# Three of four attention score blocks moved behind the expert-weight product, into the gate/value banks

## The chip, the cores and the metric

The kernel runs on one core of one Trainium2 chip. The metric is the time of one execution on the device, in microseconds. Engines are named as in the profile: PE is TensorE (PEld its weight loads), DVE VectorE, ACT ScalarE, POOL GpSimd, SP SyncE, which here issues the transfers.

## The reference

Two attentions and a SwiGLU layer. Inputs are q, k, v of 8 batches, 8 heads, 576 tokens, 64 dimensions, and p of 32 packed rows per head. All is fp32.

```python
def sm_attn(qq, kk, vv):
    s = scale * np.matmul(qq, kk.transpose(0, 1, 3, 2))
    a = np.exp(s - np.max(s, axis=-1, keepdims=True))
    return np.matmul(a / (np.sum(a, axis=-1, keepdims=True) + 1e-09), vv)
p_packed = sm_attn(p, k, v)              # first attention: 32 rows over 576 keys
out = sm_attn(q, p_packed, p_packed)     # second attention: 576 rows over 32 keys
x = out.transpose(0, 2, 1, 3).reshape(4608, 512)
g = x @ w_gate                           # 512 x 1536
result = (g * sigmoid(g) * (x @ w_val)) @ w_out   # 1536 x 512
```

## The kernel before

**Algebra.** The second attention is never multiplied out. With the weights `a2` of the second attention (576 tokens by 32 packed rows per head), gate and value are `a2` times the product of the packed rows with the gate and value weights. That product, called M, is small and is made once for each batch and each pair of chunks of the 1536 inner columns (`m_mm`). Gate and value (`gv_chunk`), and the output product (`out_mm`), run in fp32r with each operand split into a high and a low word: three matmuls replace one. The split of M is a cast on ACT (`mh`, line 513) and a subtraction on DVE that reads the same PSUM bank again (`ml`, line 487).

**Stages.** Batch 0 runs from a list of words written by hand (`PROGRAM`), with its own order. Batches 1 to 7 run in a loop (line 807). For batch b it goes through 12 chunks `fc` of 128 inner columns. In each chunk the tokens come in two parts: A (256) and B (320). A chunk writes, on PE:

1. A: gate tile, value tile (six matmuls each, line 544);
2. if `fc` is odd, M for the next pair of chunks (lines 201 and 517; in chunk 11, M of the next batch);
3. the output matmuls of the previous chunk's A (six, line 564), absent in chunk 0;
4. B: gate tile, value tile;
5. the output matmuls of the previous chunk's B, absent in chunk 0.

A counter (`fill`, line 821) steps at each tile and at each group of three output matmuls: 1 and 2 are A's two tiles, 3 and 4 the outputs of A, 5 and 6 B's tiles, 7 and 8 the outputs of B. M is written at count 2.

Beside PE, each part goes through silu of the gate tile (ACT, line 551), the product with the value tile `hf` (DVE, 556; for B also `t`, 559), a cast `hh` (ACT, 107) and a subtraction `hl` (DVE, 113).

**Attention of the next batch.** While batch b runs, the attentions of d = b + 1 are made by the generator `aux_of`. It takes a step at counts 4 and 8 of every chunk but chunk 0. The first attention (`q_scores`, `q_weights`) has two blocks of scores, g = 0 and 1, each 32 matmuls into two banks. Each bank is read by a maximum and a subtraction (lines 335 and 336). Then follow the exponential (339), sums, a gather of maxima and sums through DRAM (`zd`, then `x`), the common factor, a transpose of the weights, and the product with v (`q_pack`, 395). The second attention has two blocks of scores too (`s2_mm`), one for each half of the tokens, each 16 matmuls into two banks, read by two transposes (421). Each half then has maximum and subtraction (441, 442), exponential (446), sums (453 to 455), scaling (459), a transpose (468), a cast (471) and a subtraction (475), which give `a2` in two words.

Before the change the four blocks of scores are written at chunk 1 count 4, chunk 2 count 4, chunk 7 count 4 and chunk 7 count 8. Each stands between output matmuls and B, or between output matmuls and the next A.

**Banks.** PSUM has three pools: `acc` (four banks, the outputs), `gv` (two banks, gate and value tiles in turn) and `aux` (two banks: M, all scores, the packed product, and the outputs of the remaining tokens of two batches). In the loop `ps()` gives an `aux` bank.

**Order of the queues.** PE's order is the written order. On the other engines the compiler orders the instructions by when it takes them to be ready. An instruction that went through `pin` (line 91) is kept behind the instruction written just before it on its engine; one that did not may be issued earlier or later than where it is written. The attention's DVE instructions and exponentials are pinned. `hf`, `hh`, `hl`, silu, the casts `mh` and the low words `ml` are not. The exponentials are put in a list `late` and written behind the next silu.

Of the kernel before, what the change touches and what calls it, by code (L numbers as in the profile page):

```python
# [59 lines left out]
def tile_pack_attention_swiglu(ctx: ExitStack, tc: tile.TileContext, qT, kT, v, vq, pT, wgv, wout, out):  # L60
# [30 lines left out]
    def pin(ins):  # L91

        return tc.keep_in_program_order(ins) if steady[0] else ins

    late = []

    def ps():
        turn[0] += 1
# [210 lines left out]

    sq = {}  # L310

    def q_scores(b):


        k_t, p_t = kps[b]
        e = pool.tile([P, NPAR, NHP, NKQ * NP], F32, tag="s2", bufs=1, name="e1")
        z = pool.tile([P, 2, NPAR, NHP], F32, tag="z1", bufs=2, name="z1")
        sq[b] = (e, z)
        nc.gpsimd.memset(e[:, :, :, SQ:], 0.0)
        for g in range(2):  # L320
            pss = [ps(), ps()]
            for i in range(2):
                for j in range(NJ):
                    for par in range(NPAR):
                        r = slice(64 * par, 64 * par + 64)
                        nc.tensor.matmul(  # L326
                            pss[par][NP * j : NP * j + NP, i * SQ : (i + 1) * SQ],
                            p_t[r, 2 * g + i, :],
                            k_t[r, j // 2, 2 * g + i, j % 2 * SQ : j % 2 * SQ + SQ],
                            start=True, stop=True,  # L330
                        )
            hs = slice(2 * g, 2 * g + 2)
            for par in range(NPAR):
                x, m = pss[par][:, : 2 * SQ].rearrange("p (h n) -> p h n", h=2), z[:, 0, par, hs]
                pin(nc.vector.tensor_reduce(m, x, axis=AX.X, op=ALU.max))
                pin(nc.vector.tensor_tensor(
                    e[:, par, hs, :SQ], x, m.unsqueeze(2).broadcast_to([P, 2, SQ]), op=ALU.subtract
                ))
            late.append(lambda hs=hs: pin(nc.scalar.activation(e[:, :, hs, :SQ], e[:, :, hs, :SQ], AF.Exp, scale=SCALE)))
            yield  # L340
            if g == 0:
                yield

    def q_weights(b):


        e, z = sq[b]
        for g in range(2):
            if g:
                yield  # L350
            hs = slice(2 * g, 2 * g + 2)
            pin(nc.vector.tensor_reduce(z[:, 1, :, hs], e[:, :, hs, :SQ], axis=AX.X, op=ALU.add))
        zv = z.rearrange("p s r h -> p s (r h)")
        x = pool.tile([P, NJ, 2, H], F32, tag="x1", bufs=1, name="x1")
        zd = dram.tile([P, 2, H], F32, tag="zd", bufs=2, name="zd")
        nc.sync.dma_start(zd, zv)
        for i in range(NJ):
            nc.sync.dma_start(x[NP * i : NP * i + NP], zd.rearrange("(j n) s h -> n j s h", j=NJ))
        for _ in range(2):
            yield  # L360
        y = pool.tile([P, 3, NJ + 1, H], F32, tag="pp", bufs=1, name="y1")
        m, t, f = y[:, 2, 0], y[:, 2, 1], y[:, 2, 2]
        pin(nc.vector.tensor_reduce(m, x[:, :, 0].rearrange("p j h -> p h j"), axis=AX.X, op=ALU.max))
        pin(nc.vector.tensor_tensor(
            y[:, 0, :NJ], x[:, :, 0], m.unsqueeze(1).broadcast_to([P, NJ, H]), op=ALU.subtract
        ))
        pin(nc.vector.tensor_tensor(y[:, 0, NJ], zv[:, 0], m, op=ALU.subtract))
        late.append(lambda: pin(nc.scalar.activation(y[:, 0], y[:, 0], AF.Exp, scale=SCALE)))
        yield
        pin(nc.vector.tensor_tensor(y[:, 1, :NJ], y[:, 0, :NJ], x[:, :, 1], op=ALU.mult))  # L370
        pin(nc.vector.tensor_reduce(t, y[:, 1, :NJ].rearrange("p j h -> p h j"), axis=AX.X, op=ALU.add))
        pin(nc.vector.tensor_scalar(f, t, 1e-9, None, op0=ALU.add))
        pin(nc.vector.reciprocal(t, f))
        pin(nc.vector.tensor_tensor(f, t, y[:, 0, NJ], op=ALU.mult))
        yield
        a1 = pool.tile([P, NPAR, NHP, NKQ, NP], F32, tag="a1", bufs=1, name="a1")
        for par in range(NPAR):
            w = e[:, par, :, :SQ]
            pin(nc.vector.tensor_tensor(
                w, w, f[:, NHP * par : NHP * par + NHP].unsqueeze(2).broadcast_to([P, NHP, SQ]), op=ALU.mult  # L380
            ))
            pin(nc.vector.transpose(
                a1[:, par].rearrange("p h k n -> p (h k n)"), e[:, par].rearrange("p h n -> p (h n)")
            ))
            yield
        sq[b] = a1

    def q_pack(b):
        a1, v_t = sq.pop(b), vs.pop(b)
        p_p = ps()  # L390
        for hp in range(NHP):
            for k in range(NKQ):
                for g in range(P // NP):
                    par, ds = g // 2, slice(g % 2 * NP, g % 2 * NP + NP)
                    nc.tensor.matmul(  # L395
                        p_p[NP * g : NP * g + NP, NP * hp : NP * hp + NP],
                        a1[:, par, hp, k, :], v_t[:, par, hp, k, ds],
                        start=(k == 0), stop=(k == NKQ - 1),
                    )
        ppts[b] = pool.tile([P, P], F32, tag="ppt", bufs=2, name="ppt")  # L400
        pin(nc.vector.transpose(ppts[b], p_p[:, :P]))
# [6 lines left out]

    two = {}

    def s2_mm(b, c):
        two[b, c] = [ps(), ps()]
        q_t, ppt = qs[b], ppts[b]
        by_head(
            [x[:, :HS] for x in two[b, c]], lambda r, hp: ppt[r, 32 * hp : 32 * hp + 32],
            lambda r, hp: q_t[r, c, hp],
        )

    def s2_block(b, c):
        for par in range(NPAR):  # L420
            pin(nc.vector.transpose(st2[b][0][:, c, par], two[b, c][par][:, :HS]))

    def s2_scores(b):
        for c in range(2):
            s2_mm(b, c)
            s2_block(b, c)
            yield

    def s2_view(b, cs):
        s2, r2 = st2[b]  # L430
# [53 lines left out]

    def m_lows():
        while lows:
            nc.vector.tensor_tensor(*lows.pop(0), op=ALU.subtract)  # L487

    m_ps = {}

# [26 lines left out]
    def m_part(b, k, fcs):  # L517
        m_mm(b, k, fcs)
        m_high(b, k, fcs)
        m_lows()  # L520

    t4 = {}

# [3 lines left out]
        split(hh, hl, src, hi, lo)  # L527
        return hh, hl

    def gv_chunk(b, fc, is_b, fill):  # L530
        odd = b % 2
        n = NB if is_b else NA
        off = (0 if odd else 256) if is_b else (320 if odd else 0)
# [15 lines left out]
            fill()  # L549
        sg = pool.tile([P, NB], F32, tag="sg", bufs=1, name="sg")  # L550
        nc.scalar.activation(sg[:, :n], pgs[0][:, :n], AF.Silu)  # L551
        if late:
            late.pop(0)()
        hf = pool.tile([P, 256], F32, tag="hf", bufs=2, name="hf")
        o, o4 = (64, 0) if is_b and odd else (0, 256)
        nc.vector.tensor_tensor(hf, pgs[1][:, o : o + 256], sg[:, o : o + 256], op=ALU.mult)  # L556
# [19 lines left out]

    both = slice(0, 2)

    def aux_of(b):

        d = b + 1
        if d == B:
            return
        yield from q_scores(d)
        yield from q_weights(d)
        if d + 1 < B:
            load_k(d + 1)
        q_pack(d)
        yield
        yield  # L590
        if d < B - 1:
            load_v(d + 1)
        s2_tiles(d)
        yield from s2_scores(d)
        if d < B - 1:
            load_q(d + 1)
        s2_a2(d)
        order = (1, 0) if d % 2 else (0, 1)
        halves = [slice(c, c + 1) for c in order]
        first, second = halves  # L600
        s2_max(d, first)
        late.append(lambda: s2_exp(d, first))
        yield
        s2_sums(d, first)
        yield
        s2_max(d, second)
        late.append(lambda: s2_exp(d, second))
        yield
        s2_scale(d, first)
        low = s2_back(d, first.start)  # L610
        yield
        low()
        s2_sums(d, second)
        yield
        s2_scale(d, second)
        low = s2_back(d, second.start)
        yield
        low()

    with tc.manual_schedule(engines={mybir.EngineType.PE}):  # L620
        warm_ps = ps_aux.tile([P, 512], F32, tag="aux", name="warm_ps")
# [184 lines left out]
        steady[0] = True  # L806
        for b in range(1, B):
            rows, accs = begin(b)
            aux = aux_of(b)
            ha, hb = {}, {}  # L810

            def outs(fc, which, fill):
# [5 lines left out]
            for fc in range(NFC):  # L818
                count = [0]

                def fill():
                    count[0] += 1
                    if count[0] == 2:
                        if fc == NFC - 1 and b + 1 < B:
                            run_all(aux)
                            m_part(b + 1, 0, both)
                        elif fc % 2 and fc + 1 < NFC:
                            m_part(b, (fc + 1) // 2, both)
                    if b == 1 and 1 <= fc <= 6 and count[0] == 7:
                        wout_high(fc + 5)  # L830
                        wout_low(fc + 5)
                    if fc and count[0] in (4, 8):
                        next(aux, None)

                ha[fc] = gv_chunk(b, fc, False, fill)
                if fc:
                    outs(fc - 1, 0, fill)
                hb[fc] = gv_chunk(b, fc, True, fill)
                if fc:
                    outs(fc - 1, 1, fill)  # L840
            run_all(aux)
            outs(NFC - 1, 0, lambda: None)
            outs(NFC - 1, 1, lambda: None)
            end(rows, accs)
# [46 lines left out]
```

## Time and profile before

| What | Value |
|---|---|
| median of 3 runs | 759.64 us (758.2 to 760.34) |
| profiled execution, whole | 760.24 us |
| profiled execution, span of its instructions | 758.5 us |
| PE busy | 745.1 us (98%) |
| PEld busy | 590.6 us (78%) |
| DVE busy | 456.6 us (60%) |
| ACT busy | 369.6 us (49%) |
| bytes moved by DMA | 59.15 MB |
| granted clock of PE, mean | 0.996 |

The whole time includes what lies around the span. Busy times count each engine alone, and they overlap. A row of a timeline gives start, length, engine, line of the kernel, operation, the tile written and those read, and a count of merged instructions; what stands in brackets is the idle time of the engine before it and whom it waited for. A row of a group gives count, total busy time and mean nanoseconds of one, and then the idle time before them.

### The profile page before, as it was taken

To read this page: it belongs to the slowest core of one execution; us is meant where nothing else is said; L and a number is where in the kernel's file an instruction comes from. 1 tells how busy PE (TensorE), PEld (TensorE's weight loads), DVE (VectorE), ACT (ScalarE), POOL (GpSimd) and SP (SyncE) were. 2 spreads that over 40 slices of the span, in tenths; PEclk is the share of its full clock that TensorE was granted. 3 is DMA by queue.
4 is the path that set the end of the run, shared out by engine and by line. 5 is a ranking of instruction groups with operands and counts; after the bars stand their busy time and mean duration, and the time that the engine had idled before them with its cause. 6 is when DMAs were issued, how large, how long until landed. Compare 5 with 4: busy or idle time off the path is not lost.

```text
span 758.5 us, 15106 instructions
## 1 busy us (share of the span) xinstructions
PE 745.1 (98%) x6280; PEld 590.6 (78%) x6280; DVE 456.6 (60%) x1004; ACT 369.6 (49%) x662; POOL 2.0 (0%) x13
## 2 busy tenths in 40 slices
PE   7999999999999999998999999999999999999998
PEld 5756666787888878787788887878788787888886
DVE  5997977665756547454674556656475554743334
ACT  3777654653626436452443545464272642633331
POOL 0000000000000000000000000000000000000000
PEclk9999999999999999999999999999999999999999
DMA  9686582203011030122201221100101000010001
GB/s 355 242 319 249 207 313 78 67 3 133 1 70 67 4 134 1 56 69 71 64 29 42 69 72 63 43 15 3 71 2 69 2 3 2 1 56 1 1 1 70
DMA packets 20004, 59.15 MB, mean 78 GB/s; under 512 B 5984, under 2 KB 7008, under 8 KB 17376
## 3 DMA queue, kind: packets, MB, share of 16 engines
q1 hardware_dynamic: 19792, 58.12, 21.2%
q8 instruction: 49, 0.80, 0.4%
q14 instruction: 19, 0.16, 0.1%
q10 hardware_dynamic: 144, 0.07, 0.0%
HBM read 48.69 MB, written 9.49 MB: 77 GB/s over the span
## 4 chain that ended last, share of the span: by engine, by line
PE 95%; DVE 2%; ACT 1%; issue 1%; ACTq 0%
PE gv L544 36%; PE acc L564 30%; PE aux L201 8%; PE gv L721 6%; PE acc L747 5%; PE aux L564 4%; PE aux L395 1%; PE aux L326 1%; DVE ml L487 1%; PE acc L625 1%; PE warm_ps L625 1%; ACT mh L513 1%; PE gv_aux L201 0%; PE aux L277 0%; DVE w L133 0%
## 5 line engine op out<-in xcount | busy, mean ns | idle before, releaser
L551 ACT ACTIVATE sg<-gv 128x256 f32<-128x256 f32 (+1 forms) x168 | 68.9, 410 | 179.7 <-PE gv L544 145.4
L544 PE MATMUL gv<-a2h,ml 128*128 128x256 f32 (+1 forms) x672 | 148.4, 302 | 0.7
L544 PE MATMUL gv<-a2h,mh 128*128 128x256 f32 (+1 forms) x672 | 144.7, 297 | 0.4 <-issue 0.4
L544 PE MATMUL gv<-a2l,mh 128*128 128x256 f32 (+1 forms) x672 | 144.4, 296 | 0.0
L556 DVE TENSOR_TENSOR hf<-gv,sg 128x256 f32<-128x256 f32 x168 | 70.7, 421 | 120.6 <-PE gv L544 101.2
L564 PE MATMUL acc<-wo_h,hl 128*128 128x512 f32 x336 | 136.8, 407 | 0.0
L564 PE MATMUL acc<-wo_l,hh 128*128 128x512 f32 x336 | 132.4, 394 | 0.0
L564 PE MATMUL acc<-wo_h,hh 128*128 128x512 f32 x336 | 131.7, 392 | 0.0
L544 PEld LDWEIGHTS gv<-a2h,ml 128*128 128x128 f32 x672 | 113.9, 189 | 21.7 <-issue 7.6
L107 ACT CAST hh<-hf 128x256 fp32r<-128x256 f32 x168 | 67.9, 404 | 120.5 <-DVE hf L556 120.4
L113 DVE TENSOR_TENSOR hl<-hf,hh 128x256 fp32r<-128x256 f32 x168 | 71.0, 423 | 80.3 <-ACT hh L107 79.8
L544 PEld LDWEIGHTS gv<-a2h,mh 128*128 128x128 f32 x672 | 109.0, 191 | 0.6 <-issue 0.6
L544 PEld LDWEIGHTS gv<-a2l,mh 128*128 128x128 f32 x672 | 108.5, 190 | 0.0
L564 PEld LDWEIGHTS acc<-wo_h,hl 128*128 128x128 f32 x336 | 63.4, 189 | 42.5 <-issue 34.4
L564 PEld LDWEIGHTS acc<-wo_h,hh 128*128 128x128 f32 x336 | 63.3, 188 | 14.6
L564 PEld LDWEIGHTS acc<-wo_l,hh 128*128 128x128 f32 x336 | 63.4, 189 | 7.7
L487 DVE TENSOR_TENSOR ml<-aux,mh 128x512 fp32r<-128x512 f32 x92 | 59.0, 683 | 6.4 <-ACT mh L513 6.3
L201 PE MATMUL aux<-w,ppt 64*32 64x512 f32 (+1 forms) x784 | 52.4, 588 | 0.5 <-ACT mh L513 0.5
L513 ACT CAST mh<-aux 128x512 fp32r<-128x512 f32 x92 | 49.2, 588 | 3.6 <-PE aux L201 0.7
L747 PE MATMUL acc<-wo_f,h 128*128 128x512 f32 x96 | 44.2, 594 | 0.0
L551 ACT ACT_TABLE_LOAD x30 | 38.5, 1283 | 4.2 <-issue 3.6
L747 PEld LDWEIGHTS acc<-wo_f,h 128*128 128x128 f32 x96 | 17.3, 189 | 17.2 <-issue 15.7
(145 smaller groups left out, 756.0 us busy)
## 6 DMA issues: line engine op xcount, KB each, us to landing
st<-in_wgv SPq DMA_DIRECT2D x12, 1024.0 KB, 6.9
k_t<-in_kT SPq DMA_DIRECT2D x16, 576.0 KB, 4.9
q_t<-in_qT SPq DMA_DIRECT2D x16, 576.0 KB, 5.0
out<-ot SPq DMA_DIRECT2D x36, 256.0 KB, 2.1
v_t<-in_vq SPq DMA_DIRECT2D x6, 1280.0 KB, 5.7
st<-in_wout SPq DMA_DIRECT2D x6, 1024.0 KB, 7.2
v_t<-in_v SPq DMA_DIRECT2D x2, 1024.0 KB, 8.3
p_t<-in_pT SPq DMA_DIRECT2D x7, 64.0 KB, 2.5
```

The source lines that it names most:

```text
L107: e.copy(dst, src)
L113: lo.tensor_tensor(dst_l, src, dst_h.bitcast(F32), op=ALU.subtract)
L201: nc.tensor.matmul(outs[par][32 * hp : 32 * hp + 32], lhs(r, hp), rhs(r, hp), start=True, stop=True)
L487: nc.vector.tensor_tensor(*lows.pop(0), op=ALU.subtract)
L513: nc.scalar.copy(m[0][at], src)
L544: nc.tensor.matmul(pg[:, :n], m_[:, g, f, s * P : (s + 1) * P], a_[:, g, off : off + n], start=(i == 0), stop=(i == 5),)
L551: nc.scalar.activation(sg[:, :n], pgs[0][:, :n], AF.Silu)
L556: nc.vector.tensor_tensor(hf, pgs[1][:, o : o + 256], sg[:, o : o + 256], op=ALU.mult)
L564: nc.tensor.matmul(acc[:, :], h_[:, c : c + P], w_[fc // 2][:, fc % 2], start=(fc == 0 and i == 0), stop=(fc == NFC - 1 and i == 2),)
L625: nc.tensor.matmul(at[:, :P], ident, ident, start=True, stop=True)
L721: nc.tensor.matmul(held[i][s][:, :n], m_[:, g, f, s * P : (s + 1) * P], a_[:, g, off : off + n], start=(j == 0), stop=(j == len(todo) - 1),)
L747: nc.tensor.matmul(accs[2 * is_b + c], half(i)[:, c * P : c * P + P], wos[fc // 2][:, fc % 2], start=(fc == 0), stop=(fc == NFC - 1),)
```

## The change

The generator becomes a table: `plan_of(b)` says, for each chunk and place, what is written there. The places are the counts 2, 4 and 8, `"a"` (behind the silu of A), `"b"` (behind the silu of B) and `"m"` (behind the whole of A, so behind M on PE in odd chunks). The functions of the attention are cut into pieces, each written as before.

- The first block of the first scores moves to chunk 0, count 2. It stays in `aux`.
- The second moves to chunk 1, `"m"`, and takes its two banks from `gv`.
- The second attention's blocks move to chunk 7, `"m"` and chunk 9, `"m"`, and take their banks from `gv`. The order of its two halves on PE is now that of their use.
- `m_lows` (the subtractions `ml`) moves from behind M's casts to behind whatever stands at `"m"`, and is pinned.
- The exponentials move from B to A: chunks 1, 2, 4, 8 and 10. Sums, gather, common factor, the packed product's turn, maxima and the scaling of the second attention move by up to two chunks, as the table says. The loads of k and p are written at chunk 3 count 8 in place of chunk 6 count 4, that of v in the same chunk 7, that of q in chunk 9 in place of chunk 8.

```diff
+    def gv_ps():
+        return ps_gv.tile([P, 512], F32, tag="gv", name="gv_aux")
+
-    def q_scores(b):
+    def q_scores(b, g, bank=ps):
...
+        pss = [bank(), bank()]
...
-    def s2_mm(b, c):
-        two[b, c] = [ps(), ps()]
+    def s2_mm(b, c, bank=ps):
+        two[b, c] = [bank(), bank()]
...
     def m_lows():
         while lows:
-            nc.vector.tensor_tensor(*lows.pop(0), op=ALU.subtract)
+            pin(nc.vector.tensor_tensor(*lows.pop(0), op=ALU.subtract))
...
     def m_part(b, k, fcs):
         m_mm(b, k, fcs)
         m_high(b, k, fcs)
-        m_lows()
...
-    def gv_chunk(b, fc, is_b, fill):
+    def gv_chunk(b, fc, is_b, fill, behind):
...
-        if late:
-            late.pop(0)()
+        behind()
...
-    def aux_of(b):
...
+    def plan_of(b):
+        d, plan = b + 1, {}
+        def at(fc, place, *todo):
+            plan.setdefault((fc, place), []).extend(todo)
+        if d < B:
+            c, c2 = (1, 0) if d % 2 else (0, 1)
+            cs, cs2 = slice(c, c + 1), slice(c2, c2 + 1)
+            at(0, 2, lambda: q_scores(d, 0))
+            at(1, "a", lambda: q_exp(d, 0))
+            at(1, "m", lambda: q_scores(d, 1, gv_ps))
+            at(1, 8, lambda: q_sums(d, 0))
+            at(2, "a", lambda: q_exp(d, 1))
+            at(2, 8, lambda: q_sums(d, 1), lambda: q_gather(d))
+            at(3, 8, lambda: q_common(d))
+            if d + 1 < B:
+                at(3, 8, lambda: load_k(d + 1))
+            at(4, "a", lambda: q_common_exp(d))
+            at(4, 4, lambda: q_factors(d))
+            at(4, 8, lambda: q_turn(d, 0))
+            at(5, 8, lambda: q_turn(d, 1))
+            at(6, 4, lambda: q_pack(d))
+            if d + 1 < B:
+                at(7, "m", lambda: load_v(d + 1))
+            at(7, "m", lambda: s2_tiles(d), lambda: s2_a2(d))
+            at(7, "m", lambda: s2_mm(d, c, gv_ps), lambda: s2_block(d, c))
+            at(7, 8, lambda: s2_max(d, cs))
+            at(8, "a", lambda: s2_exp(d, cs))
+            at(8, 8, lambda: s2_sums(d, cs), lambda: s2_scale(d, cs), lambda: s2_turn(d, c), lambda: s2_high(d, c))
+            at(9, "m", lambda: s2_mm(d, c2, gv_ps), lambda: s2_block(d, c2))
+            if d + 1 < B:
+                at(9, "m", lambda: load_q(d + 1))
+            at(9, 4, lambda: s2_low(d, c))
+            at(9, 8, lambda: s2_max(d, cs2))
+            at(10, "a", lambda: s2_exp(d, cs2))
+            at(10, 8, lambda: s2_sums(d, cs2), lambda: s2_scale(d, cs2), lambda: s2_turn(d, c2))
+            at(10, 8, lambda: s2_high(d, c2))
+            at(11, 4, lambda: s2_low(d, c2))
+        return lambda fc, place: [f() for f in plan.pop((fc, place), ())]
...
                     count[0] += 1
                     if count[0] == 2:
+                        run(fc, 2)
                         if fc == NFC - 1 and b + 1 < B:
-                            run_all(aux)
                             m_part(b + 1, 0, both)
                         elif fc % 2 and fc + 1 < NFC:
                             m_part(b, (fc + 1) // 2, both)
...
-                ha[fc] = gv_chunk(b, fc, False, fill)
+                ha[fc] = gv_chunk(b, fc, False, fill, lambda: run(fc, "a"))
+                run(fc, "m")
+                m_lows()
                 if fc:
                     outs(fc - 1, 0, fill)
-                hb[fc] = gv_chunk(b, fc, True, fill)
+                hb[fc] = gv_chunk(b, fc, True, fill, lambda: run(fc, "b"))
```

More of the change, by code (lines that the diff above doesn't have):

```diff
@@ L93, in pin @@
         return tc.keep_in_program_order(ins) if steady[0] else ins
-    late = []
     def ps():
@@ L310, in tile_pack_attention_swiglu @@
     sq = {}
-    def q_scores(b):
+    def gv_ps():
+        return ps_gv.tile([P, 512], F32, tag="gv", name="gv_aux")
+    def q_scores(b, g, bank=ps):
         k_t, p_t = kps[b]
[L316 to L342, printed above, removed]
@@ L344, in q_weights @@
-    def q_weights(b):
-        e, z = sq[b]
[L348 to L353, printed above, removed]
+        if g == 0:
+            e = pool.tile([P, NPAR, NHP, NKQ * NP], F32, tag="s2", bufs=1, name="e1")
+            z = pool.tile([P, 2, NPAR, NHP], F32, tag="z1", bufs=2, name="z1")
+            sq[b] = [e, z]
+            nc.gpsimd.memset(e[:, :, :, SQ:], 0.0)
@@ new lines, in q_scores @@
+        e, z = sq[b]
+        pss = [bank(), bank()]
+        for i in range(2):
+            for j in range(NJ):
+                for par in range(NPAR):
+                    r = slice(64 * par, 64 * par + 64)
+                    nc.tensor.matmul(
+                        pss[par][NP * j : NP * j + NP, i * SQ : (i + 1) * SQ],
+                        p_t[r, 2 * g + i, :],
+                        k_t[r, j // 2, 2 * g + i, j % 2 * SQ : j % 2 * SQ + SQ],
+                        start=True, stop=True,
+                    )
@@ new lines, in q_scores, with q_exp @@
+        hs = slice(2 * g, 2 * g + 2)
+        for par in range(NPAR):
+            x, m = pss[par][:, : 2 * SQ].rearrange("p (h n) -> p h n", h=2), z[:, 0, par, hs]
+            pin(nc.vector.tensor_reduce(m, x, axis=AX.X, op=ALU.max))
+            pin(nc.vector.tensor_tensor(
+                e[:, par, hs, :SQ], x, m.unsqueeze(2).broadcast_to([P, 2, SQ]), op=ALU.subtract
+            ))
+    def q_exp(b, g):
+        x = sq[b][0][:, :, 2 * g : 2 * g + 2, :SQ]
+        pin(nc.scalar.activation(x, x, AF.Exp, scale=SCALE))
@@ L354, in q_weights, with q_sums, q_gather @@
+    def q_sums(b, g):
+        e, z = sq[b]
+        hs = slice(2 * g, 2 * g + 2)
+        pin(nc.vector.tensor_reduce(z[:, 1, :, hs], e[:, :, hs, :SQ], axis=AX.X, op=ALU.add))
+    def q_gather(b):
         x = pool.tile([P, NJ, 2, H], F32, tag="x1", bufs=1, name="x1")
         zd = dram.tile([P, 2, H], F32, tag="zd", bufs=2, name="zd")
-        nc.sync.dma_start(zd, zv)
+        nc.sync.dma_start(zd, sq[b][1].rearrange("p s r h -> p s (r h)"))
         for i in range(NJ):
             nc.sync.dma_start(x[NP * i : NP * i + NP], zd.rearrange("(j n) s h -> n j s h", j=NJ))
-        for _ in range(2):
-            yield
+        sq[b].append(x)
@@ L361, in q_weights, with q_common @@
+    def q_common(b):
+        _, z, x = sq[b]
         y = pool.tile([P, 3, NJ + 1, H], F32, tag="pp", bufs=1, name="y1")
-        m, t, f = y[:, 2, 0], y[:, 2, 1], y[:, 2, 2]
+        sq[b].append(y)
+        m = y[:, 2, 0]
         pin(nc.vector.tensor_reduce(m, x[:, :, 0].rearrange("p j h -> p h j"), axis=AX.X, op=ALU.max))
@@ L366, in q_weights, with q_common_exp, q_factors @@
         ))
-        pin(nc.vector.tensor_tensor(y[:, 0, NJ], zv[:, 0], m, op=ALU.subtract))
-        late.append(lambda: pin(nc.scalar.activation(y[:, 0], y[:, 0], AF.Exp, scale=SCALE)))
-        yield
+        pin(nc.vector.tensor_tensor(y[:, 0, NJ], z.rearrange("p s r h -> p s (r h)")[:, 0], m, op=ALU.subtract))
+    def q_common_exp(b):
+        y = sq[b][3]
+        pin(nc.scalar.activation(y[:, 0], y[:, 0], AF.Exp, scale=SCALE))
+    def q_factors(b):
+        _, _, x, y = sq[b]
+        t, f = y[:, 2, 1], y[:, 2, 2]
         pin(nc.vector.tensor_tensor(y[:, 1, :NJ], y[:, 0, :NJ], x[:, :, 1], op=ALU.mult))
@@ L374, in q_weights, with q_turn @@
         pin(nc.vector.tensor_tensor(f, t, y[:, 0, NJ], op=ALU.mult))
[L375 to L386, printed above, removed]
+    def q_turn(b, par):
+        e, f = sq[b][0], sq[b][3][:, 2, 2]
+        if par == 0:
+            sq[b].append(pool.tile([P, NPAR, NHP, NKQ, NP], F32, tag="a1", bufs=1, name="a1"))
+        w = e[:, par, :, :SQ]
+        pin(nc.vector.tensor_tensor(
+            w, w, f[:, NHP * par : NHP * par + NHP].unsqueeze(2).broadcast_to([P, NHP, SQ]), op=ALU.mult
+        ))
+        pin(nc.vector.transpose(
+            sq[b][4][:, par].rearrange("p h k n -> p (h k n)"), e[:, par].rearrange("p h n -> p (h n)")
+        ))
     def q_pack(b):
-        a1, v_t = sq.pop(b), vs.pop(b)
+        a1, v_t = sq.pop(b)[4], vs.pop(b)
         p_p = ps()
@@ L421, in s2_block @@
             pin(nc.vector.transpose(st2[b][0][:, c, par], two[b, c][par][:, :HS]))
[L423 to L427, printed above, removed]
     def s2_view(b, cs):
@@ L577, in tile_pack_attention_swiglu @@
     both = slice(0, 2)
-    def aux_of(b):
[L581 to L618, printed above, removed]
+    def plan_of(b):
[36 more added lines that the diff above has]
+        return lambda fc, place: [f() for f in plan.pop((fc, place), ())]
@@ L808, in tile_pack_attention_swiglu @@
             rows, accs = begin(b)
-            aux = aux_of(b)
+            run = plan_of(b)
             ha, hb = {}, {}
@@ L831, in fill @@
                         wout_low(fc + 5)
-                    if fc and count[0] in (4, 8):
-                        next(aux, None)
-                ha[fc] = gv_chunk(b, fc, False, fill)
+                    if count[0] in (4, 8):
+                        run(fc, count[0])
+                ha[fc] = gv_chunk(b, fc, False, fill, lambda: run(fc, "a"))
+                run(fc, "m")
+                m_lows()
                 if fc:
                     outs(fc - 1, 0, fill)
-                hb[fc] = gv_chunk(b, fc, True, fill)
+                hb[fc] = gv_chunk(b, fc, True, fill, lambda: run(fc, "b"))
                 if fc:
                     outs(fc - 1, 1, fill)
-            run_all(aux)
             outs(NFC - 1, 0, lambda: None)
```

## The prediction

> **What bounds the kernel now.** I read the page's head first, then the table by stretches for whole batches, then the waits of TensorE, then the timelines of one batch (b = 4), engine by engine.
>
> ```profile
> span 758.5 us, 15106 instructions
> PE 745.1 (98%) x6280; PEld 590.6 (78%) x6280; DVE 456.6 (60%) x1004; ACT 369.6 (49%) x662; POOL 2.0 (0%) x13
> ```
>
> The table by stretches, one stretch from the end of one batch's work on TensorE to the end of the next (columns: length, busy us and instructions of each engine, granted clock, DMA share, GB/s):
>
> ```profile
> 307.17:396.24 89.07, 86.87 (x785) 70.92 (x785) 51.46 (x121) 43.23 (x79) 0.20 (x1) 0.98 0.17 55
> 404.40:489.69 85.29, 85.09 (x787) 69.36 (x786) 50.12 (x117) 42.72 (x78) 0.20 (x1) 1.00 0.15 51
> ```
>
> TensorE (PE) is the bound: busy 98%, and 85.09 of 85.29 us in batch 4. Only what shortens TensorE's own stream counts; DVE (60%) and ACT (49%) matter where TensorE waits for them. Busy hides small losses, because the ends of matmuls are modelled, so I go by starts. Waits of the weight loads (PEld) and of PE show who is waited for:
>
> ```profile
> PEld aux L201 <- DVE ml L487: 4.6, 12, 0.4
> PEld aux L326 <- DVE ml L487: 4.6, 12, 0.4
> PE aux L395 <- issue: 2.0, 1, 2.0
> ```
>
> Twelve waits each at L326 (scores of the first attention) and L201 (here the scores of the second): two in each of six blocks, always for `ml`, M's low words, still reading the `aux` banks. The third row is one hole in batch 3, which also has the clock of 0.98 and is 3.8 us longer than batch 4. PE, chunks 1 and 2 of batch 4 (start, us, engine, line, operation, count):
>
> ```profile
> 407.45 0.40 PE L544 MATMUL gv<-a2h,ml 128*128 128x256 f32 x2
> ...
> 408.42 0.47 PE L544 MATMUL gv<-a2h,ml 128*128 128x256 f32 x2
> ...
> 409.30 1.09 PE L201 MATMUL aux<-w,ppt 64*32 64x512 f32 x16
> 410.32 0.50 PE L564 MATMUL acc<-wo_h,hl 128*128 128x512 f32 x1
> ...
> 411.58 0.40 PE L564 MATMUL acc<-wo_h,hh 128*128 128x512 f32 x1
> 411.91 1.25 PE L326 MATMUL aux<-k_t,p_t 64*32 64x144 f32 x32
> 413.09 0.56 PE L544 MATMUL gv<-a2h,ml 128*128 128x320 f32 x2
> ...
> 414.07 0.46 PE L544 MATMUL gv<-a2h,ml 128*128 128x320 f32 x2
> ...
> 414.95 0.39 PE L564 MATMUL acc<-wo_h,hl 128*128 128x512 f32 x1
> ...
> 416.34 0.40 PE L544 MATMUL gv<-a2h,ml 128*128 128x256 f32 x2
> ...
> 417.77 0.40 PE L564 MATMUL acc<-wo_h,hl 128*128 128x512 f32 x1
> ...
> 419.25 0.72 PE L326 MATMUL aux<-k_t,p_t 64*32 64x144 f32 x32
> 419.90 0.41 PE L544 MATMUL gv<-a2h,ml 128*128 128x320 f32 x1
> ```
>
> By starts: an A chunk (two tiles of gate and value) takes 1.43 us (416.34 to 417.77), one tile 0.72; a B tile 0.88 (414.07 to 414.95); the six output matmuls 1.39 (414.95 to 416.34), 0.23 each; M 1.02 (409.30 to 410.32). The same block of scores takes 1.18 us behind a fresh M (411.91 to 413.09) and 0.65 without one (419.25 to 419.90).
>
> **What the change removes.** It acts for d = b + 1 in batches b = 1 to 6, so each term counts six times.
>
> The stall on `ml`: 1.18 - 0.65 = 0.53 us. It stands once in the first attention and, by the equal waits at L201, once in the second. The first scores go to chunk 0, where the `aux` banks are long read; the others leave `aux`. Gain 2 x 0.53 = 1.06 us a batch.
>
> The borders between 64*32 and 128*128 matmuls: the last output matmul before the scores lasts 0.33 instead of 0.23 (411.58 to 411.91), the first tile behind them 0.98 instead of 0.88 (413.09 to 414.07): 0.20 us for a block standing alone. Three of the four blocks now stand directly behind M, which has its two borders anyway: 3 x 0.20 = 0.60 us. The seam M to scores does not occur in this trace; between 0 (both rows say 64*32) and 0.20 (a border like the others) I take 0, because what distinguishes the rows at each border with 0.10 is the array shape, and it stays. The Trainium skill, "TensorEngine Tiling (Array Packing)", Tiling Modes, Key Properties, says that changing the tiling mode, not just the tile, drains the array. By that rule the seam costs 0 and the gain is 0.60; a drain at every new block of operands would leave nothing of it.
>
> Together 1.66 us a batch, 10.0 us in six.
>
> **What it adds.** No arithmetic. The instructions moved are the same 32 or 16 matmuls, four reductions and subtractions, exponentials, and the transfers with them. A scores block moves ahead of the six output matmuls; the reading of its banks then lies under those, 1.39 us.
>
> Chunk 0 has no output matmuls, and its A and B tiles follow one another through two banks. DVE and ACT rows of batch 4:
>
> ```profile
> 406.83 0.42 DVE L113 TENSOR_TENSOR hl<-hf,hh 128x256 fp32r<-128x256 f32 x1 [0.47 <-ACT hh L107]
> 407.72 0.42 DVE L556 TENSOR_TENSOR hf<-gv,sg 128x256 f32<-128x256 f32 x1 [0.46 <-PE gv L544]
> 408.06 0.21 DVE L559 TENSOR_TENSOR t<-gv,sg 128x64 f32<-128x64 f32 x1
> ...
> 413.24 0.46 DVE L335 TENSOR_REDUCE z<-aux 128x2 f32<-128x288 f32 x1 [0.85 <-PE aux L326]
> 413.73 0.46 DVE L336 TENSOR_TENSOR e<-aux,z 128x288 f32<-128x288 f32 x1
> ...
> 414.58 0.46 DVE L336 TENSOR_TENSOR e<-aux,z 128x288 f32<-128x288 f32 x1
> 415.22 0.42 DVE L556 TENSOR_TENSOR hf<-gv,sg 128x256 f32<-128x256 f32 x1 [0.18 <-PE gv L544]
> ```
>
> ```profile
> 408.49 0.38 ACT L551 ACTIVATE sg<-gv 128x256 f32<-128x256 f32 x1
> 409.94 0.40 ACT L107 CAST hh<-hf 128x256 fp32r<-128x256 f32 x1 [1.06 <-DVE hf L556]
> 410.48 1.07 ACT L513 CAST mh<-aux 128x512 fp32r<-128x512 f32 x2
> ...
> 414.79 1.28 ACT L339 ACT_TABLE_LOAD   x1
> 416.08 0.68 ACT L339 ACTIVATE e<-e 128x576 f32<-128x576 f32 x1
> 416.67 0.39 ACT L107 CAST hh<-hf 128x256 fp32r<-128x256 f32 x1
> ```
>
> Already before, chunk 1's second A tile came 0.97 instead of 0.72 us after the first (407.45 to 408.42): 0.25 us of waiting for `hf` and `t` to read the value bank (407.72 to 408.27). Now, from chunk 0's start: A to 1.43, scores 1.53 to 2.18, B 2.28 to 4.04. DVE can read from 2.43 (413.24 is 0.15 behind 413.09); four reads take 1.80 (413.24 to 415.04), `hl` of A 0.42, so DVE is free at 4.65, while `hf` of B could start at 4.31 (407.72 is 0.27 behind 407.45). Loss 0 if `hf` slips in between, 0.34 if not. I take 0.34, since the others are written ahead of it.
>
> Chunk 1, the scores in the gate and value banks: from M's start, M to 1.02, scores to 1.67, outputs 1.77 to 3.16, then B needs the gate bank. Its reading is pinned behind `hl` of A, that waits for `hh`, and `hh` now has the exponential of the first scores ahead of it. Silu at -0.81 (408.49 against 409.30), exponential with its table load 1.98 (414.79 to 416.77), so to 1.55; `hh` to 1.95, `hl` to 2.40, the two reads of the gate bank 0.95 (413.24 to 414.19) to 3.35, and 0.15 to the matmul (408.27 to 408.42): 3.50, a wait of 0.34. If silu is not held back while M comes 0.34 later, it is nothing. I take 0.25. The value bank is asked for 0.88 later and read 0.91 later: no further wait. `ml` is late next: behind the reads, it ends near 5.6, while chunk 2, its first user, starts at 3.50 + 1.76 + 1.39 = 6.65.
>
> Chunks 7 and 9 read with two transposes in place of four instructions, and without an exponential ahead: no wait in 7. In chunk 9 the transpose of the first half, written at the end of chunk 8, can stand in front of them:
>
> ```profile
> L468 DVE STREAM_TRANSPOSE t<-s 128x576 f32<-128x576 f32 x14 | 10.8, 774 | 0.3
> k_t<-in_kT SPq DMA_DIRECT2D x16, 576.0 KB, 4.9
> ```
>
> Between 0 and 0.77 I take 0.11: most of it lies under the 1.39 us of outputs. On SP the gather through `zd` and the loads of k, p, v and q change places by one to three chunks; k lands after 4.9 us and is read a batch (85 us) later, so they cost nothing; if the gather came late, its readers would hold DVE, and by the order of the rows above then `hf`. POOL's memset only goes along.
>
> Sum: 1.66 - 0.34 - 0.25 - 0.11 = 0.96 us a batch, 5.8 us in six. The profiled execution took 760.24 us (1.7 around its span) and would take 754.4; it lies 0.6 above the median of the three runs, 759.64, so I forecast 753.8 us.
>
> **Rivals.** *Casts ahead of `hh`.* In chunk 1 M's two casts, written ahead of silu, may stand in front of `hh` on ACT when the exponential ends. ACT rows of chunks 3 and 9 show both orders:
>
> ```profile
> 425.85 1.07 ACT L513 CAST mh<-aux 128x512 fp32r<-128x512 f32 x2
> 426.81 0.42 ACT L107 CAST hh<-hf 128x256 fp32r<-128x256 f32 x1
> ```
>
> ```profile
> 469.60 0.41 ACT L107 CAST hh<-hf 128x256 fp32r<-128x256 f32 x1 [0.49 <-DVE hf L556]
> 469.91 1.07 ACT L513 CAST mh<-aux 128x512 fp32r<-128x512 f32 x2
> ```
>
> Then the wait at the gate bank is 0.25 + 1.07 = 1.32, the batch loses 0.11, and the time is 760.3 us. Against it: in chunk 1 before, `hh` came first (409.94, 410.48).
>
> *No new wait.* DVE slips `hf` in and ACT takes `hh` before the exponential: the whole 10.0 us, 749.6. Against it: in chunk 1 `hh` stood behind the exponential though `hf` ended at 415.64 (416.67).
>
> *Order as written: slower.* The first scores' reads are written before chunk 0's `hf`. If DVE's queue keeps that order, `hf` of A starts at 2.43 + 1.80 = 4.23, ends at 4.65, and B's second tile, due at 3.16, starts at 4.80: 1.64 lost, in place of the 0.34 there; on ACT the same order puts the casts first, 1.32. The batch loses 1.64 + 1.32 + 0.11 - 1.66 = 1.41: 768.1 us. It decides from 1.66 us of such waits a batch. Against it: M's casts too are written before silu and `hf`'s cast, and came behind both (408.49, 409.94, 410.48). The Trainium skill, "PSUM — Partial Sum Buffer", Engine vs sequencer instructions, calls the queues of ScalarE and VectorE strict FIFO: nothing could then repair such an order on the chip, and the time would be this one. The trace agrees as far as `hh` stays 1.03 us behind the exponential.
>
> **How the numbers follow.** Chances: forecast 0.66, casts first 0.14, no new wait 0.10, order as written 0.10. The forecast's own range is 750.5 to 757.5: the two waits at their bounds are some 3.5 us in six batches, and the hole of batch 3 can move or go (3.8 us either way, one place). The range reaches to the whole gain and nearly to the casts: 749.5 to 760.0. About 0.3%, 2.3 us, is what a measurement can tell. Faster: 0.61 of the forecast, the 0.10 without waits and some of the casts' 0.14, 0.74. Same: 0.05 of the forecast and most of the casts, 0.14. Slower: order as written and the casts' rest, 0.12.
>
> **What would show it.** Right: both waits on `ml` are gone; in chunks 1, 7 and 9 scores start 1.02 us behind M and take 0.65; a batch takes about 84.3 us instead of 85.29. Waits of the gate/value tiles (L544) for the scores' reads stay under 0.4 us each. Wrong: 1.3 us of waiting before chunk 1's B tile with two casts ahead of `hh`; B's second tile in chunk 0 waiting 1.6 us; a 0.1 us gap between M and the scores; or silu in chunks 8 to 11 so late behind its table load that a gate bank holds TensorE.

## The result, and the profile after

The changed kernel takes 751.53 us (median of 4 runs, 750.76 to 752.13); the kernel before, beside it on the same chip, 759.99 us (758.2 to 760.95). The ratio is 0.9891, 95% interval 0.9869 to 0.9913: about 8 us faster. The forecast was 753.8 us.

The head of the page, span and the engines' busy time:

```profile
span 750.2 us, 15126 instructions
PE 735.1 (98%) x6280; PEld 592.6 (79%) x6280; DVE 454.3 (61%) x1004; ACT 371.5 (50%) x662; POOL 2.0 (0%) x13
```

The work is the same 6280 matmuls; PE is still the bound, and the span is 8.3 us shorter (758.5 to 750.2). The table by stretches, first batch 3, then the outputs of the remaining tokens, then batch 4 (columns as before: length, busy us of the engines, granted clock, DMA share, GB/s):

```profile
304.82:390.18 85.36, 83.86 (x785) 70.14 (x784) 51.05 (x121) 43.66 (x79) 0.20 (x1) 1.00 0.17 58
390.18:398.55 8.37, 8.37 (x37) 6.78 (x36) 3.52 (x9) 0.59 (x1) 0.00 (x0) 1.00 0.30 112
398.55:482.86 84.31, 83.68 (x786) 70.04 (x784) 49.65 (x117) 43.08 (x78) 0.20 (x1) 1.00 0.15 51
```

Batch 4 takes 84.31 us instead of 85.29: 0.98 less, where 0.96 was forecast. Batch 3 takes 85.36 instead of 89.07, more than the change was to bring; that is taken up below. The waits of PEld and PE after:

```profile
PEld gv L547 <- DVE s L431: 3.3, 6, 0.7
...
PE gv L547 <- DVE t L561: 1.5, 4, 0.4
PE gv L547 <- issue: 1.5, 1, 1.5
...
PE aux L405 <- issue: 1.2, 1, 1.2
```

The two rows for `ml` (4.6 us each) are gone. New is a wait of the gate tile for `s`, the transposes that read the second attention's scores (six times, once a batch), and a wait for `t`, the last reader of the value bank. A row of PEld counts that queue's idle time; what PE loses is smaller (0.55 us each here, where PE loses 0.25 by starts, see below). The two rows without a cause ("issue") are holes in batches 2 and 3: stretches in which PE starts nothing and the profile shows nothing that it waits for. PE in chunks 0 and 1 of batch 4 (start, us, engine, line, operation, count):

```profile
398.55 0.40 PE L547 MATMUL gv<-a2h,ml 128*128 128x256 f32 x2
...
400.06 0.72 PE L328 MATMUL aux<-k_t,p_t 64*32 64x144 f32 x32
400.71 0.56 PE L547 MATMUL gv<-a2h,ml 128*128 128x320 f32 x2
...
402.57 0.40 PE L547 MATMUL gv<-a2h,ml 128*128 128x256 f32 x2
...
403.89 0.47 PE L547 MATMUL gv<-a2h,ml 128*128 128x256 f32 x2 [0.44 <-DVE t L561]
...
404.76 1.09 PE L199 MATMUL aux<-w,ppt 64*32 64x512 f32 x16
405.65 0.75 PE L328 MATMUL gv_aux<-k_t,p_t 64*32 64x144 f32 x32
406.33 0.50 PE L566 MATMUL acc<-wo_h,hl 128*128 128x512 f32 x1
...
408.08 0.53 PE L547 MATMUL gv<-a2h,ml 128*128 128x320 f32 x2
408.45 0.46 PE L547 MATMUL gv<-a2l,mh 128*128 128x320 f32 x2
408.74 0.46 PE L547 MATMUL gv<-a2h,mh 128*128 128x320 f32 x2
```

The first scores run at once in chunk 0 (0.65 us, 400.06 to 400.71). Chunk 1's second A tile comes 1.32 us after the first (402.57 to 403.89) where it was 0.97 before: 0.35 lost. M starts at 404.76 and the second scores already at 405.65, 0.88 us later, not 1.02. The six outputs and the wait behind them take 1.76 (406.33 to 408.08; unrounded starts), where chunk 7, without a wait there, takes 1.50: 0.26 lost. The tile behind this wait is 0.08 late as well: its first two matmuls take 0.37 (408.08 to 408.45), the next pair 0.29. DVE and ACT of the same stretch show who was late:

```profile
400.24 0.42 DVE L558 TENSOR_TENSOR hf<-gv,sg 128x256 f32<-128x256 f32 x1 [0.80 <-PE gv L547]
401.14 0.42 DVE L111 TENSOR_TENSOR hl<-hf,hh 128x256 fp32r<-128x256 f32 x1 [0.47 <-ACT hh L105]
401.48 0.45 DVE L337 TENSOR_REDUCE z<-aux 128x2 f32<-128x288 f32 x1
...
403.20 0.41 DVE L558 TENSOR_TENSOR hf<-gv,sg 128x256 f32<-128x256 f32 x1
...
406.65 0.42 DVE L111 TENSOR_TENSOR hl<-hf,hh 128x256 fp32r<-128x256 f32 x1 [1.29 <-ACT hh L105]
407.00 0.45 DVE L337 TENSOR_REDUCE z<-gv_aux 128x2 f32<-128x288 f32 x1
407.48 0.46 DVE L338 TENSOR_TENSOR e<-gv_aux,z 128x288 f32<-128x288 f32 x1
```

```profile
404.35 1.28 ACT L344 ACT_TABLE_LOAD   x1
405.64 0.69 ACT L344 ACTIVATE e<-e 128x576 f32<-128x576 f32 x1
406.23 0.39 ACT L105 CAST hh<-hf 128x256 fp32r<-128x256 f32 x1
406.53 1.06 ACT L517 CAST mh<-aux 128x512 fp32r<-128x512 f32 x2
```

In chunk 0 the row of the scores ends at 400.78, but DVE starts reading it at 401.48: `hl` stands ahead and waits 0.47 us for `hh`. `hf` of B follows the four reads and starts at 403.20, which is 4.65 us from the batch's start. In batch 3, which starts at 304.82, DVE takes the first read ahead of `hl`:

```profile
307.16 0.46 DVE L337 TENSOR_REDUCE z<-aux 128x2 f32<-128x288 f32 x1 [0.21 <-PE aux L328]
307.53 0.41 DVE L111 TENSOR_TENSOR hl<-hf,hh 128x256 fp32r<-128x256 f32 x1
...
309.12 0.42 DVE L558 TENSOR_TENSOR hf<-gv,sg 128x256 f32<-128x256 f32 x1
```

There `hf` of B starts 4.30 us from the batch's start, and chunk 1's second A tile comes 0.97 us after the first, as before the change.

In chunk 1 of batch 4 the chain is silu, table load, exponential, `hh` (406.23), `hl` (406.65), reads of the gate bank (407.00 to 407.94), B (408.08): the forecast's order, with the casts behind `hh`. Chunk 9, DVE and then PE:

```profile
462.49 0.77 DVE L472 STREAM_TRANSPOSE t<-s 128x576 f32<-128x576 f32 x1
463.18 0.81 DVE L431 STREAM_TRANSPOSE s<-gv_aux 128x288 f32<-128x288 f32 x2
```

```profile
461.92 0.51 PE L566 MATMUL acc<-wo_h,hl 128*128 128x512 f32 x1
...
463.68 0.56 PE L547 MATMUL gv<-a2h,ml 128*128 128x320 f32 x2
464.08 0.45 PE L547 MATMUL gv<-a2l,mh 128*128 128x320 f32 x2
```

The turn of the first half (L472) stands ahead of the two transposes that would free the gate bank. Outputs and wait take 1.75 (461.92 to 463.68), 0.25 more than in chunk 7, and the first pair behind the wait 0.40 instead of 0.29: 0.36 in all.

### The profile page after: what moved, and what is told of

Its sections match the earlier page's. It is cut to its first block, busy times and chain, and to the rows that moved or that the text cites. A ratio compares the mean times of both kernels' runs of the same rounds, so it can differ in the third digit from the quotient of the medians.

```text
span 750.2 us, 15126 instructions
## 1 busy us (share of the span) xinstructions
PE 735.1 (98%) x6280; PEld 592.6 (79%) x6280; DVE 454.3 (61%) x1004; ACT 371.5 (50%) x662; POOL 2.0 (0%) x13
## 4 chain that ended last, share of the span: by engine, by line
PE 85%; DVE 7%; ACT 4%; issue 1%; DMA 0%; DVEq 0%; ACTq 0%
PE gv L547 31%; PE acc L566 27%; PE aux L199 6%; PE gv L726 6%; PE acc L752 6%; PE aux L566 4%; DVE hf L558 1%; PE aux L405 1%; DVE hl L111 1%; ACT L554 1%; ACT L450 1%; ACT hh L105 1%; PE gv_aux L199 1%; PE acc L630 1%; DVE s L446 1%
```

## The experiments

**The changed kernel once more**, to see whether the holes stay.

> The changed kernel once more, nothing edited. 751.5 us if the gain is in the program. The holes of TensorE in the small matmuls of the packed product (1.45 us in batch 3, 1.73 us at the tile behind it in batch 2 of the first profile): if they belong to the program, they come again in the same two batches with the same length; if they come by chance, in other batches, or none.

Measured 751.65 us (751.16 to 752.01), ratio 0.9889 (0.9872 to 0.9905). The holes are again in chunk 6 of batches 2 and 3: between the gate tile and the value tile of B in batch 2, in the packed product in batch 3. By starts batch 3's took 1.44 us in both executions, batch 2's 1.62 and then 1.06. Their places are the same in both; the length of one is not.

**New places, old banks.** All blocks at the new places but in `aux`; `ml` is unpinned and ahead of the scores, since the scores now overwrite its bank.

```diff
-            at(1, "m", lambda: q_scores(d, 1, gv_ps))
+            at(1, "m", lambda: q_scores(d, 1))
...
-            at(7, "m", lambda: s2_mm(d, c, gv_ps), lambda: s2_block(d, c))
+            at(7, "m", lambda: s2_mm(d, c), lambda: s2_block(d, c))
...
-            at(9, "m", lambda: s2_mm(d, c2, gv_ps), lambda: s2_block(d, c2))
+            at(9, "m", lambda: s2_mm(d, c2), lambda: s2_block(d, c2))
...
-            pin(nc.vector.tensor_tensor(*lows.pop(0), op=ALU.subtract))
+            nc.vector.tensor_tensor(*lows.pop(0), op=ALU.subtract)
...
-                run(fc, "m")
                 m_lows()
+                run(fc, "m")
```

> The new places without the new banks: all four blocks of scores in the aux banks, with M's low words written ahead of them. My theory (the gate/value banks are what lets the scores follow M at once): the scores wait until casts and low words have read M's banks, some 2.6 us in chunk 1 and 2.0 in chunks 7 and 9 for each of six batches, less the two waits of 0.26 that vanish: about 36 us more than the changed kernel, 787 us (780 to 794). Rival (what counts is the borders saved by standing behind M): within 2 us of 751.5.

Measured 815.42 us. PE's waits in it, and chunk 9 of batch 4:

```profile
PE aux L199 <- DVE ml L491: 23.3, 12, 2.7
PE aux L328 <- DVE ml L491: 13.1, 11, 2.0
```

```profile
500.79 1.80 PE L199 MATMUL aux<-q_t,ppt 64*32 64x288 f32 x16 [2.38 <-DVE ml L491]
...
503.12 0.63 PE L566 MATMUL acc<-wo_l,hh 128*128 128x512 f32 x1
503.54 0.63 PE L566 MATMUL acc<-wo_h,hh 128*128 128x512 f32 x1
```

The theory holds in kind and the rival does not, but the time lies 28 us above the expected 787. PE's idle time in these rows, 23.3 + 13.1 = 36.4 us, is close to the 36 us that were expected, but it isn't the whole stall: a block of scores also stands still between its own matmuls. By starts the six batches are 63 us longer than in the changed kernel. M and scores take 4.37 us in chunk 1 (1.56 in the changed kernel) and 3.79 in chunk 7 (1.51), where the matmuls keep their speed, and 5.20 in chunk 9 (1.50), where the scores do not. With chunk 9's scores at the 1.24 us that a block takes in the other two, and less the 0.70 us of waits that vanish, an estimate of the stall is 46 us; chunk 9's share was put too low. The other 17 us or so follow the pauses: behind the one of 2.38 us the output matmuls come 0.42 us apart instead of 0.23, at a granted clock of 0.50 (503 to 505). The mean granted clock of this kernel is 0.971, against 0.997. Without the other banks the new places are the worst of all versions tried.

**New banks, old places.** The kernel before, with three blocks in the gate/value banks.

```diff
+    def gv_ps():
+        return ps_gv.tile([P, 512], F32, tag="gv", name="gv_aux")
...
-            pss = [ps(), ps()]
+            pss = [gv_ps(), gv_ps()] if g else [ps(), ps()]
...
-        two[b, c] = [ps(), ps()]
+        two[b, c] = [gv_ps(), gv_ps()] if b > 1 else [ps(), ps()]
```

> The kernel before with three of the four blocks in the gate/value banks, but at their old places behind the output matmuls. My theory (the six output matmuls must lie between the scores and the next user of the bank): the stall on low words at the second attention goes (0.53 us a batch), but the tile behind each block waits for its reading, 1.1 us in chunk 2, 0.75 twice in chunk 7: 2.1 us a batch slower, 772 us (767 to 777). Rival (leaving the aux banks is the gain): 0.53 us a batch less than before, 757 us.

Measured 774.21 us. At the old places the tile directly behind the scores waits for the reading; chunk 2 of batch 4:

```profile
427.50 0.46 DVE L339 TENSOR_TENSOR e<-gv_aux,z 128x288 f32<-128x288 f32 x1
...
428.11 0.53 PE L547 MATMUL gv<-a2h,ml 128*128 128x320 f32 x2 [1.18 <-DVE e L339]
```

Each of these two kernels ran once, and the kernel before took 760.4 us beside them: places alone lose 55 us and banks alone 13.8. For the three blocks that change their bank, places and banks gain only together: the outputs between scores and B are the cover for the reading.

**The first block alone.** The kernel before, with only the first scores moved to chunk 0 and their exponential behind the silu of chunk 1.

```diff
             if g == 0:
                 yield
+                yield
...
-        if late:
+        if late and fc:
...
                     if count[0] == 2:
+                        if fc == 0:
+                            next(aux, None)
```

> The kernel before with one step of the change: the first block of scores in chunk 0, its exponential behind chunk 1's first silu; the others at their old places in aux. My theory: the stall of 0.53 us goes, the wait of chunk 1's second A tile grows by 0 to 0.35: 0.2 to 0.5 us a batch, 757.5 us (756 to 759). Rival (the stall only moves to the next user of the aux banks): 760.

Measured 757.47 us (one run). In batch 4 (85.14 us) chunk 1's scores and their 0.53 of stall are gone, and the second A tile comes after 1.32 us, as in the full change.

**`ml` not pinned.** The full change, but the compiler may put `ml` where it likes.

```diff
-            pin(nc.vector.tensor_tensor(*lows.pop(0), op=ALU.subtract))
+            nc.vector.tensor_tensor(*lows.pop(0), op=ALU.subtract)
```

> The changed kernel with M's low words not pinned. The order of the queues then has both low words of chunk 1, and one each in chunks 7 and 9, ahead of the reading of the gate/value banks. My theory: the B tile behind waits longer, 1.3 us in chunk 1, 0.1 in chunk 7, 0.6 in chunk 9: 2.0 us a batch, 763.5 us (760 to 766). Rival (low words are off the path, the pin does nothing): 751.5.

Measured 763.16 us (762.71 to 763.45), ratio to the kernel before 1.0044 (1.0027 to 1.0062): slower than without any change. Chunk 1 of batch 4, DVE and then PE:

```profile
411.93 1.29 DVE L491 TENSOR_TENSOR ml<-aux,mh 128x512 fp32r<-128x512 f32 x2
413.13 0.45 DVE L337 TENSOR_REDUCE z<-gv_aux 128x2 f32<-128x288 f32 x1
```

```profile
414.22 0.53 PE L547 MATMUL gv<-a2h,ml 128*128 128x320 f32 x2 [1.45 <-DVE e L338]
```

`ml` goes ahead of the reads, and B waits 1.45 us; outputs and wait take 3.11 instead of 1.76. The pin is worth 763.16 - 751.6 = 11.6 us, more than the whole gain.

**The first exponential behind `hh`.** The full change, with the exponential of the first block written at `"m"` in chunk 1.

```diff
-            at(1, "a", lambda: q_exp(d, 0))
+            at(1, "m", lambda: q_exp(d, 0))
```

> The changed kernel with one exponential (first block, chunk 1) written behind the cast of A's h instead of behind silu. My theory: the 0.26 us at chunk 1's B tile is the time that this cast spends behind the exponential and its table load; it goes, with the 0.08 on the tile behind it: 0.33 us a batch, 749.5 us (748.5 to 750.5). Rival (DVE's four reads alone are too long for the six output matmuls): 751.5.

Measured 749.71 us (749.63 to 750.06), ratio 0.9865 (0.9846 to 0.9883). ACT, chunk 1 of batch 4:

```profile
404.21 0.41 ACT L105 CAST hh<-hf 128x256 fp32r<-128x256 f32 x1 [1.07 <-DVE hf L558]
404.64 1.28 ACT L344 ACT_TABLE_LOAD   x1
```

`hh` comes first, and outputs and wait take 1.49 instead of 1.76. The exponential ahead of `hh` was the cause of that wait.

**The first block behind B's tiles**, on top of that edit: chunk 0, count 4 in place of 2, so that its reading does not stand ahead of `hf` of B.

```diff
-            at(0, 2, lambda: q_scores(d, 0))
+            at(0, 4, lambda: q_scores(d, 0))
```

> The same, and the first block of scores moves from between A and B of chunk 0 to behind B. My theory: the wait of chunk 1's second A tile (0.25 to 0.60 by batch, and 0.07 on the tile behind) is DVE reading scores ahead of the product of B; with the scores behind B it goes altogether, because they also cover that product: 0.5 us a batch on top, 746.5 us (745 to 748). Rival (DVE is full there, the wait moves to the gate bank of chunk 1): 749.5 to 751.5.

Measured 752.27 us (751.65 to 752.46), ratio 0.9896 (0.9877 to 0.9915), where 746.5 was expected: this theory failed. Chunk 1 of batch 4:

```profile
401.18 0.72 PE L328 MATMUL aux<-k_t,p_t 64*32 64x144 f32 x32
401.83 0.50 PE L547 MATMUL gv<-a2h,ml 128*128 128x256 f32 x2
...
402.64 0.40 PE L547 MATMUL gv<-a2h,ml 128*128 128x256 f32 x2
...
403.68 1.72 PE L199 MATMUL aux<-w,ppt 64*32 64x512 f32 x9 [0.16 <-DVE e L338]
...
406.27 0.50 PE L566 MATMUL acc<-wo_h,hl 128*128 128x512 f32 x1
```

The wait that was aimed at is gone: the second A tile comes after 0.81 us. The rival was wrong too, since the gate bank of chunk 1 isn't waited for. But the first scores stand in `aux`, and the next user of `aux` is M. From M's start to the outputs it now takes 2.59 (403.68 to 406.27) in place of 1.57 (404.76 to 406.33). The block itself runs 1.8 us later in its batch (401.18 from a batch start of 397.87, against 400.06 from 398.55), so its banks come free later too, and the wait went from the tile to M, where it costs more.

**That, and chunk 9's turn behind the transposes.**

```diff
-            at(8, 8, lambda: s2_sums(d, cs), lambda: s2_scale(d, cs), lambda: s2_turn(d, c), lambda: s2_high(d, c))
-            at(9, "m", lambda: s2_mm(d, c2, gv_ps), lambda: s2_block(d, c2))
+            at(8, 8, lambda: s2_sums(d, cs), lambda: s2_scale(d, cs))
+            at(9, "m", lambda: s2_mm(d, c2, gv_ps), lambda: s2_block(d, c2), lambda: s2_turn(d, c), lambda: s2_high(d, c))
```

> The same two edits, and the transpose of the second attention's first half written behind the reading of the second half's scores in chunk 9. My theory: chunk 9's wait of 0.26 and the 0.10 on the tile behind go too: 744.5 us (743 to 746). Rival (the late transpose makes the next step of the second attention late, and its silu): 746.5 or more.

Measured 749.39 us (749.24 to 751.68), ratio 0.9866 (0.9847 to 0.9885). Against the kernel above it is 2.9 us, where 2.0 was expected for the turn; the miss against 744.5 is the first block's, carried along.

**The turn alone**, the last edit on the full change and nothing else.

> The kernel after, with the first half's transpose and cast (turn, high words) written in chunk 9 behind the transposes that read the second half's scores, instead of at the end of chunk 8. If the wait of chunk 9 (0.26 us at the B tile and 0.10 at the tile behind it, batch 4) comes from that one DVE instruction standing ahead of the transposes, both go and nothing follows, since the low words of the half are used a batch later: 751.5 - 6 x 0.36 = 749.4 us. If the wait has another cause (the transposes only go behind a cast), 751.5.

Measured 749.56 us (748.7 to 750.13), ratio 0.9872 (0.9849 to 0.9895). Chunk 9 of batch 4, DVE:

```profile
461.16 0.84 DVE L431 STREAM_TRANSPOSE s<-gv_aux 128x288 f32<-128x288 f32 x2
461.93 0.73 DVE L472 STREAM_TRANSPOSE t<-s 128x576 f32<-128x576 f32 x1
```

Outputs and wait take 1.50, and the tile behind them its 0.88. The one transpose in front was the cause of both excesses.

**Exponential and turn together**, with the first block left at count 2.

> The kernel after, with two edits: the first block's exponential written behind A of chunk 1 (alone 749.7 us), and the first half's turn behind the transposes in chunk 9. The first scores stay in chunk 0, count 2. If the two waits are independent, the gains add: 749.7 - 6 x 0.36 = 747.6 us. If the turn's gain is eaten by another wait, as the first block's move was by M's banks, 749.7, and the gap between the two kernels with the first block moved (752.3 and 749.4) was the spread of other holes.

Measured 746.54 us (746.36 to 746.97), ratio 0.9833 (0.9815 to 0.9851). The interval lies below that of the change as it was (0.9869 to 0.9913): this is the best version, 5.0 us faster than the change and 2.9 faster than the next (749.39). The two gains add. By starts chunk 1 gains 0.34 us a batch and chunk 9 0.36, in batch 6 0.54, together 4.4 us; the holes of batches 2 and 3 are 0.26 and 0.32 shorter than in the change's profile, which no edit explains.

## Why the prediction was right

The mechanism of the gain held: the stalls and borders that the change was to remove are gone, at the forecast's size. That the net of batch 4 came out so near is partly luck: three terms were mis-sized and cancelled, and a fourth, chunk 0's, has its size for another reason than the forecast's. Batch 4, in us gained a batch:

| term | forecast | measured |
|---|---|---|
| stall on `ml` | 1.06 | 1.06: both rows of waits gone |
| three blocks without borders of their own | 0.60 | 0.60 |
| seam from M to scores | 0 (0 to -0.20) | +0.14 each, +0.42 |
| chunk 0's reading ahead of `hf` | -0.34 | -0.35 (0 in batches 1 and 3, -0.12 in 5) |
| chunk 1, gate bank | -0.25 (to -0.34) | -0.34 (0.26 and 0.08 behind it) |
| chunk 9, turn ahead of transposes | -0.11 (to -0.77) | -0.36 (0.25 and 0.10 behind it, rounded) |
| sum | 0.96 | 1.03 |

The batch itself is 0.98 shorter; 0.07 is lost in its last 18 output matmuls, which take 4.18 instead of 4.11. Of the signs named beforehand, the waits on `ml` and the length of a batch (84.31 for 84.3) came as forecast. The scores start 0.88 us behind M, not 1.02. The waits of a tile for the scores' reads stay at 0.26 us by starts, under the 0.4 that was named, except in chunk 9 of batch 6 (0.43).

**Seam.** The step that took 0 failed, and its bounds did too: they ran from a loss to nothing, and there is a gain. The row of M lasts 1.09 from 404.76, to 405.85, and the scores start at 405.65; in front of output matmuls the next start was 1.02 behind M's. The forecast carried that 1.02 over, but it was measured in front of a block of another shape, so a part of the border behind M was already in it. The scores themselves take 0.68, 0.63 and 0.62 in chunks 1, 7 and 9 instead of 0.65, so a seam gains 0.10 to 0.17, the three 0.43. That the array shape, not the block, sets a border was right. The Trainium skill, "TensorEngine Tiling (Array Packing)", Tiling Modes, Key Properties, has only changes of the mode drain the array; the trace agrees at this seam.

**Waits.** A wait cost more than its own length: the first pair of matmuls behind it takes 0.08 to 0.10 longer (0.37 and 0.40 for 0.29), as behind a border (400.71 to 401.11, 0.40). Neither chunk 1's nor chunk 9's term had this part. In chunk 9 the transpose in front was named and its cover overrated; moving it away returned the whole term.

**Chunk 0.** That the size is right in batches 2, 4 and 6 is luck, because the mechanism was another. The forecast had the four reads first, from 2.43, and added 1.80 for them and 0.42 for `hl`, which makes `hf` of B 0.34 late. In batch 3 the first read does come first, at 2.34, and the others ahead of `hf`, and nothing is lost: the four reads and `hl` take 1.96 by starts (307.16 to 309.12), not 2.22, since an instruction can start up to 0.1 us before the row of the one ahead ends, and `hf` starts at 4.30, where the forecast put it without any wait (4.31). Batch 1 is the same, and batch 5, with the same order, loses 0.12. In batches 2, 4 and 6 `hl` stands ahead of all reads, and DVE idles 0.47 for `hh`: that is the 0.35. So the loss comes from `hl`, not from the reads, and an order with the first read ahead of `hl` in every batch should win back some 1 us (estimate: three times 0.35). No run tried it.

**Rivals.** Casts ahead of `hh` did not happen (406.23, then 406.53). No new wait happened at one of three places, chunk 0, in batches 1 and 3. The order as written did not come, since chunk 0's `hf` (400.24) went ahead of the reads (401.48). What an unlucky order can cost was seen at another instruction: with `ml` unpinned it is 11.6 us. The Trainium skill, "PSUM — Partial Sum Buffer", Engine vs sequencer instructions, calls the queue of VectorE strict FIFO; DVE's idling in front of `hl`, while the scores, whose row ends at 400.78, are read only from 401.48, agrees.

**The whole.** By starts the six batches gain 2.39, -0.02, 3.71, 0.98, 1.28 and 0.74 us, 9.1 together. Of these, 2.4 stand in chunk 6, where both kernels have holes. They were 0.91 in batch 1, 0.65 in batch 2 and 2.21 in batch 3, there with 1.5 us of matmuls at half speed behind it (granted clock 0.57 from 353 to 356); now they are none, 1.62 and 1.44, and the half speed does not come. Outside chunk 6 the batches gain 6.7, against the 5.8 of the forecast, mainly because chunk 0's loss stays away in batches 1 and 3. The outputs of the remaining tokens lost 0.2 in each of four places, 0.8 us. 6.7 + 2.4 - 0.8 = 8.3, the span's gain. So the 2.5 us by which it exceeds 5.8 are 0.9 of mis-sized terms and 2.4 of holes, less those 0.8. The forecast's range allowed for the holes; its sum did not, and what makes them stays open.

## What to carry to other kernels

A bank that is read late is a wait for its next user, so moving work into other banks pays only where something else, here six output matmuls, stands between writing and the next user; name that user for every place tried, or the wait comes back elsewhere. In a queue that is kept in order one unpinned instruction of the shared engine (here `ml`) can cost more than the whole change gains. Small waits are then worth chasing one by one: two moved lines gave another 5 us. And a term that comes out right in one batch is checked in the others, and by its mechanism: chunk 0's was right by its number alone.

## What the runs showed of the hardware that was not expected

- The block behind M starts 0.14 us earlier where it has M's array shape than where it has another (0.88 and 1.02), and a wait for a bank costs 0.08 to 0.10 us beyond itself. The hole of batch 2 in the changed kernel does not: the first pair behind it takes 0.29.
- Pauses of 1.45 to 2.38 us were followed by stretches of matmuls at half speed (output matmuls 0.42 us apart instead of 0.23), but not in every batch. With the new places in the old banks they came behind the pause of chunk 9 (2.38 us) in all six batches, behind that of chunk 1 (2.04) in three and behind that of chunk 7 (1.45) in two; before the change one came behind the hole of batch 3 (2.21 by starts). In the changed kernel none came behind the holes (1.62 and 1.44).
- The 36 output matmuls of the remaining tokens take longer in some programs. Before the change, as after it in the kernel with the first block behind B, the stretch is:

```profile
396.07:404.24 8.17, 8.17 (x38) 6.76 (x36) 3.48 (x9) 0.59 (x1) 0.00 (x0) 1.00 0.31 116
```

In every kernel with the first scores at count 2 of chunk 0 it is 8.36 or 8.37, and in the four others 8.15 to 8.17, the last batch included, which has no scores beside it. The last 18 output matmuls of a batch differ the same way, 4.18 and 4.11. The 0.2 us are some 6 ns on each of 36 matmuls, at a granted clock of 1.00. The cause is open; that in the last batch no scores run speaks against the work beside them.
